# One weight product of a fused attention and bilinear kernel in float32r split parts instead of float32

## The chip, the cores and the metric

The kernel runs on one core of a Trainium2 chip. The metric is the device time of one execution in microseconds (us), the median of three runs. The engines are PE (matrix products), DVE (vector operations), ACT (scalar engine: copies, activations), POOL and SP. SP issues the loads from HBM, ACT issues the stores.

## The reference

An attention block with 8 batches, 8 heads, 512 tokens, 32 state rows and 64 elements per head runs in both directions; its result, 544 rows of 512 per batch, goes through a bilinear block.

```python
scores = scale * x @ state.T;  a = softmax(scores);   xread = a @ state      # 512 rows per batch
scores2 = scale * state @ x.T; a2 = softmax(scores2); sread = a2 @ x         # 32 rows per batch
x = concatenate([xread, sread]) as rows of 512                               # 8 * 544 rows
h = (x @ w1) * (x @ w2) @ w3                                                 # 512 -> 1024 -> 1024
out = h @ w_out                                                              # 1024 -> 512
```

x and state are float32, the four weights come as float64.

## The kernel before

`w3 @ w_out` doesn't depend on x, so the kernel forms it once (`wo`, 8 tiles of 128 rows by 512, `FT` = 8) and multiplies `g = (x @ w1) * (x @ w2)` by it. Large products run in float32r: an operand is split into `hi` (rounded to float32r by a copy on ACT) and `lo` (the rest, a subtraction on DVE), and three products hi·lo, hi·hi, lo·hi are summed. `split` writes such a pair. The product `w3 @ w_out` alone runs on whole float32 operands.

The program has these parts, in this order:

- **Weights.** `to_f32` loads one chunk of 128 x 1024 float64 numbers into a `raw` buffer (SP, 1 MB) and turns their bits into float32: two passes on ACT (line 100 into the destination, line 102 into `ulps`) and two on DVE (lines 103 and 104). There are 20 chunks: 4 of w_out (`convert_wout`), 8 of w3 (`convert_w3`, one for each tile of `wo`) and 8 of w1 and w2 (`convert_quarter`, two for each of four quarters, kept in `w_sb`). Chunks of w_out and the first four of w3 lie in places of `w_sb` that w1 and w2 take later.
- **`w34(i, ks)`** forms tile i of `wo`: eight products 128 x 128 by 128 x 512 (one for each k), summed in a PSUM bank, then split into `wo_hi` and `wo_lo`.
- **Attention of batch 0**, between the tiles of `wo`: `scores` (line 115 on PE, then a chain of DVE and ACT passes up to `at_hi`, `at_lo`), `transpose_a2` (line 185, copied by line 187) and `read_state` (line 197, whose result is scaled into `sread` by eight small ACT operations, line 205).
- **Stage 1 of batch 0** (`stage1`, line 256, 8 tiles of g) by quarters: `sets(q)` multiplies the state by quarter q of w1 and w2 (`sw_hi`, `sw_lo`; line 115), stage 1 multiplies that by `at`; `hidden` makes the product of the two halves and splits it into g. `early_stage2` runs part of stage 2 for two row tiles in between.
- **Stage 2** (`stage2`, `project`, line 266): g by `wo`, four row tiles per batch; the next batch's attention and `sw` (`side_steps`) stand between them.
- **Batches 1 to 7** repeat stage 1 and stage 2. Before the last one, `state_rows` does both stages for the 256 state rows of all batches; its inputs are transposed `sread` (line 408) and split parts of `w_sb` (`grp_z`).

PE and SP run their instructions in the order in which they are written. ACT and DVE are ordered by a scheduler when the program is built, and then run strictly in that order. PSUM has two single banks (`bank`) for `wo` and stage 2 and three double ones (`two_banks`).

Of the kernel before, what the change touches and what calls it, by code (L numbers as in the profile page):

```python
# [21 lines left out]
F32 = mybir.dt.float32  # L22
# [6 lines left out]
P = 128  # L29
NF = 512  # L30
# [3 lines left out]
def attn_bilinear_kernel(  # L34
# [46 lines left out]

    def split(hi, lo, src):

        nc.scalar.copy(out=hi, in_=src)  # L84
        nc.vector.tensor_tensor(out=lo, in0=src, in1=hi.bitcast(F32), op=ALU.subtract)  # L85


    def to_f32(pool, src, out):

        raw = pool.tile([P, NW], mybir.dt.int64, name="raw", bufs=3)
        nc.sync.dma_start(out=raw, in_=src)
        words = raw.bitcast(I32).rearrange("p (n k) -> p k n", k=2)
        high, low = words[:, 1], words[:, 0]
        bits = out.bitcast(I32)
        nc.scalar.activation(out=out, in_=high.bitcast(F32), func=AF.Prelu, scale=2.0**-112, alpha=-(2.0**32))  # L100
        ulps = pool.tile([P, NW], I32, name="ulps", bufs=2)
        nc.scalar.activation(out=ulps, in_=low.bitcast(U32), func=AF.Copy, scale=2.0**-29)  # L102
        nc.vector.tensor_scalar(out=bits, in0=bits, scalar1=3, scalar2=None, op0=ALU.logical_shift_left)
        nc.vector.tensor_tensor(out=bits, in0=bits, in1=ulps, op=ALU.add)  # L104
# [29 lines left out]
    def attention_steps(b):  # L134
        xd = x_tiles[b][0]
        a2 = {}

        def scores():
            ps = two_banks()
            per_head(ps, b, lambda rows, j: xd[rows, j])  # L140
            flat = lambda t: t.rearrange("p k s -> p (k s)")

            s1 = work_tile()
            nc.vector.transpose(out=flat(s1), in_=flat(ps))  # L144

            m2 = att.tile([P, KT], F32, name="m2")
            nc.vector.tensor_reduce(out=m2, in_=ps, axis=AX.X, op=ALU.max)
            nc.vector.tensor_scalar_mul(m2, m2, -SCALE)
            e2 = att.tile([P, KT, S], F32, name="e2", bufs=1)
            sum2 = att.tile([P, KT], F32, name="sum2")  # L150
            for kt in range(KT):
                one = slice(kt, kt + 1)
                nc.scalar.activation(
                    out=e2[:, kt], in_=ps[:, kt], func=AF.Exp, bias=m2[:, one], scale=SCALE, accum_out=sum2[:, one]
                )
            nc.vector.tensor_scalar_add(sum2, sum2, 1e-9)
            nc.vector.reciprocal(out=sum2, in_=sum2)
            a2["e"], a2["sum"] = e2, sum2

            J = KT * S // NS  # L160
            s1v = flat(s1).rearrange("p (j n) -> p j n", n=NS)
            m1 = att.tile([P, J], F32, name="m1")
            nc.vector.tensor_reduce(out=m1, in_=s1v, axis=AX.X, op=ALU.max)
            nc.vector.tensor_tensor(
                out=s1v, in0=s1v, in1=m1.unsqueeze(2).broadcast_to([P, J, NS]), op=ALU.subtract
            )
            nc.scalar.activation(out=s1, in_=s1, func=AF.Exp, scale=SCALE)
            sum1 = att.tile([P, J], F32, name="sum1")
            nc.vector.tensor_reduce(out=sum1, in_=s1v, axis=AX.X, op=ALU.add)  # L169
            nc.vector.tensor_scalar_add(sum1, sum1, 1e-9)  # L170
            nc.vector.reciprocal(out=sum1, in_=sum1)
            nc.vector.tensor_tensor(
                out=s1v, in0=s1v, in1=sum1.unsqueeze(2).broadcast_to([P, J, NS]), op=ALU.mult
            )
            at = work_tile()
            nc.vector.transpose(out=flat(at), in_=flat(s1))
            at_tiles[b] = [att.tile([P, KT, S], F32R, name=f"at_{part}", bufs=1) for part in ("hi", "lo")]
            split(*at_tiles[b], at)

        def transpose_a2():  # L180
            ps = two_banks()
            for kt in range(KT):
                for t in range(NT):
                    ts = slice(t * P, (t + 1) * P)
                    nc.tensor.transpose(out=ps[:, kt, ts], in_=a2["e"][:, kt, ts], identity=ident)  # L185
            a2["t"] = work_tile()
            nc.scalar.copy(out=a2["t"], in_=ps)

        def read_state():

            xs = x_tiles[b][1]
            ps = two_banks()
            for kt in range(KT):
                for t in range(NT):
                    for j in range(NP):
                        mine = slice(j * NS, (j + 1) * NS)
                        nc.tensor.matmul(  # L197
                            ps[mine, kt, :D], a2["t"][:, kt, t * P + j * NS:t * P + (j + 1) * NS],
                            xs[:, t, 2 * j + kt], start=(t == 0), stop=(t == NT - 1),
                        )  # L200
            rows = slice(b % PER * NS, (b % PER + 1) * NS)
            for kt in range(KT):
                for j in range(NP):
                    mine = slice(j * NS, (j + 1) * NS)
                    nc.scalar.activation(
                        out=sread[rows, b // PER, 2 * j + kt, :], in_=ps[mine, kt, :D],
                        func=AF.Copy, scale=a2["sum"][mine, kt:kt + 1],
                    )

        return scores, transpose_a2, read_state  # L210

# [23 lines left out]
        split(*(t[:, :, c * NQ:(c + 1) * NQ] for t in tiles[half, i]), ps)  # L235


    def hidden(ps, n, g_hi, g_lo):
        a_sb = main.tile([P, NF], F32, name="tmp", bufs=4)
        nc.scalar.copy(out=a_sb[:, :n], in_=ps[:, 0, :n])  # L240
        nc.vector.tensor_tensor(out=a_sb[:, :n], in0=a_sb[:, :n], in1=ps[:, 1, :n], op=ALU.mult)  # L241
        split(g_hi, g_lo, a_sb[:, :n])

    def new_g():
        return [main.tile([P, NF], F32R, name=f"g_{part}", bufs=FT) for part in ("hi", "lo")]

    def stage1(b, ft, gs):
        half, c = divmod(ft * P, NF)
        ps = two_banks()
        hi, lo = at_tiles[b]  # L250
        for i in range(2):
            w_hi, w_lo = sw_tiles[b][half, i]
            k = 0
            for kt in range(KT):
                for w, a in ((w_hi, lo), (w_hi, hi), (w_lo, hi)):
                    nc.tensor.matmul(  # L256
                        ps[:, i], w[:, kt, c:c + P], a[:, kt], start=(k == 0), stop=(k == 3 * KT - 1)
                    )
                    k += 1
        gs.append(new_g())  # L260
        hidden(ps, S, *gs[-1])

    def project(ps, gs, tt, ft):
# [26 lines left out]
    def run(steps):  # L290
        for step in steps:
            step()
# [9 lines left out]

    with tc.tile_pool(name="pro", bufs=2) as pro:

        places = [w_sb[:, n // 2, n % 2].rearrange("p j f -> p (j f)") for n in range(2 * QT)]
        w_out = places[FT // 2:]
        w3s, w34_ps = {}, {}

        def convert_wout(j):
            to_f32(pro, wout[j], w_out[j])  # L310

        def convert_w3(i):
            w3s[i] = places[i] if i < FT // 2 else pro.tile([P, NW], F32, name="w3", bufs=2)
            to_f32(pro, w3t[i], w3s[i])

        def w34(i, ks):

            if ks[0] == 0:
                w34_ps[i] = bank()
            ps = w34_ps[i]  # L320
            for k in ks:
                nc.tensor.matmul(  # L322
                    ps[:, :DO], w3s[i][:, k * P:(k + 1) * P], w_out[k // 2][:, k % 2 * DO:(k % 2 + 1) * DO],
                    start=(k == 0), stop=(k == FT - 1),
                )
            if ks[-1] == FT - 1:
                split(wo["hi"][:, i], wo["lo"][:, i], ps[:, :DO])

# [29 lines left out]
                w34(i, ks[2 * j:2 * j + 2])  # L358
        for i in range(2, FT):
            convert_w3(i)  # L360
            w34(i, ks)
            if i == 2:
                load_x(0)
                scores, transpose_a2, read_state = attention_steps(0)
# [9 lines left out]
                convert_quarter(1)  # L374
        for quarter in range(QT):
            stage1(0, 2 * quarter, gs)
            if quarter + 2 < QT:
                convert_quarter(quarter + 2)
            if quarter + 1 < QT:
                sets(quarter + 1)  # L380
            else:
                run(side[0][:1])
            if quarter:
                early_stage2(quarter - 1)
            if quarter == 1:
                load_x(1)
                side = side_steps(1)
            stage1(0, 2 * quarter + 1, gs)
        run(side[0][1:])
        early_stage2(QT - 1)  # L390
        for tt in range(NT):
            dests = [(out[0, tt * P:(tt + 1) * P], 0, P)]
# [9 lines left out]
    def state_rows():  # L402
# [10 lines left out]
        for ft in range(FT):  # L413
            quarter, c = divmod(ft * P, NQ)
            ps = two_banks()
            for i in range(2):
# [4 lines left out]
                for kt in range(NP):  # L421
                    ks = slice(kt * P, (kt + 1) * P)
                    hi, lo = (t[:, kt] for t in sr)
                    for w, a in ((wh, lo), (wh, hi), (wl, hi)):
# [1 line left out]
                            ps[:, i, :n], w[:, ks], a, start=(k == 0), stop=(k == 3 * NP - 1)  # L426
                        )
                        k += 1
            gs.append([g[:, :n] for g in new_g()])
            hidden(ps, n, *gs[-1])  # L430
        for tt in range(n // P):
            stage2(gs, tt, [(out[tt * PER + q, S:], q * NS, NS) for q in range(PER)])
# [1 line left out]

    for b in range(1, B):
        if b == B - 1:
            state_rows()
        gs = []
        for ft in range(FT):
            stage1(b, ft, gs)  # L440
# [43 lines left out]
```

## Time and profile before

| | |
|---|---|
| median of 3 runs | 526.55 us (526.3 to 529.43) |
| profiled execution | 526.63 us |
| its span, first to last instruction | 524.8 us |
| PE busy | 502.5 us, 96% |
| DVE, ACT busy | 266.2 us (51%), 247.2 us (47%) |
| moved by DMA | 47.67 MB, mean 91 GB/s |

PE's busy time has modelled ends, so the places where another engine keeps PE waiting are found in the waits and in the chain of work that ended last. The first 84 us hold all work on the weights; after them the batches repeat.

### The profile page before, as it was taken

To read this page: it belongs to the slowest core of one execution; us is meant where nothing else is said; L and a number is where in the kernel's file an instruction comes from. 1 tells how busy PE (TensorE), PEld (TensorE's weight loads), DVE (VectorE), ACT (ScalarE), POOL (GpSimd) and SP (SyncE) were. 2 spreads that over 40 slices of the span, in tenths; PEclk is the share of its full clock that TensorE was granted. 3 is DMA by queue.
4 is the path that set the end of the run, shared out by engine and by line. 5 is a ranking of instruction groups with operands and counts; after the bars stand their busy time and mean duration, and the time that the engine had idled before them with its cause. 6 is when DMAs were issued, how large, how long until landed. Compare 5 with 4: busy or idle time off the path is not lost.

```text
span 524.8 us, 7504 instructions
## 1 busy us (share of the span) xinstructions
PE 502.5 (96%) x3192; PEld 369.8 (70%) x3192; DVE 266.2 (51%) x352; ACT 247.2 (47%) x403; POOL 0.7 (0%) x6
## 2 busy tenths in 40 slices
PE   1999898999999999999999999999999999999996
PEld 0444346756886788678868886887688777998885
DVE  3648948376155724653464348343915492742410
ACT  5657966245443634453444434443544364632410
POOL 0000000000000000000000000000000000000000
PEclk9999899999999999999999999999999999999999
DMA  8987733021302120321023003300330001001001
GB/s 328 387 335 315 283 136 149 5 81 61 106 0 101 50 97 2 101 101 46 0 106 122 21 1 121 106 21 0 121 121 1 21 22 41 0 1 41 0 33 49
DMA packets 11361, 47.67 MB, mean 91 GB/s; under 512 B 1344, under 2 KB 2368, under 8 KB 6720
## 3 DMA queue, kind: packets, MB, share of 16 engines
q1 hardware_dynamic: 6336, 38.28, 19.7%
q10 hardware_dynamic: 4992, 8.92, 4.6%
q8 instruction: 25, 0.41, 0.3%
q14 instruction: 8, 0.07, 0.0%
HBM read 38.27 MB, written 8.91 MB: 90 GB/s over the span
## 4 chain that ended last, share of the span: by engine, by line
PE 88%; DVE 5%; DMA 3%; ACT 3%; issue 1%; DVEq 0%; ACTq 0%
PE ps_o L266 35%; PE ps L256 32%; PE ps_o L322 7%; PE ps L115 6%; PE ps L425 4%; PE ps L197 2%; PE ps L185 1%; DMA raw<-in_w3t_dram 1%; DMA raw<-in_wout_dram 1%; DMA raw<-in_w_dram 1%; ACT ulps L102 1%; DVE w_sb L104 1%; ACT w_sb L100 1%; DVE sum L169 0%; DVE work L144 0%
## 5 line engine op out<-in xcount | busy, mean ns | idle before, releaser
L266 PE MATMUL ps_o<-wo_lo,g_hi 128*128 128x512 f32 x272 | 108.6, 399 | 1.0 <-ACT g_hi L84 1.0
L241 DVE TENSOR_TENSOR tmp<-tmp,ps 128x512 f32<-128x512 f32 (+1 forms) x72 | 47.3, 657 | 118.6 <-ACT tmp L240 118.6
L266 PE MATMUL ps_o<-wo_hi,g_lo 128*128 128x512 f32 x272 | 106.1, 390 | 0.6 <-DVE g_lo L85 0.6
L266 PE MATMUL ps_o<-wo_hi,g_hi 128*128 128x512 f32 x272 | 106.0, 390 | 0.0
L256 PE MATMUL ps<-at_lo,sw_hi 128*128 128x512 f32 x256 | 100.2, 392 | 1.7 <-DVE tmp L241 1.7
L256 PE MATMUL ps<-at_hi,sw_lo 128*128 128x512 f32 x256 | 99.6, 389 | 0.0
L256 PE MATMUL ps<-at_hi,sw_hi 128*128 128x512 f32 x256 | 99.6, 389 | 0.0
L240 ACT COPY tmp<-ps 128x512 f32<-128x512 f32 (+1 forms) x72 | 40.5, 562 | 63.9 <-PE ps L256 63.0
L85 DVE TENSOR_TENSOR g_lo<-tmp,g_hi 128x512 fp32r<-128x512 f32 (+1 forms) x72 | 47.6, 661 | 41.6 <-ACT g_hi L84 41.5
L84 ACT CAST g_hi<-tmp 128x512 fp32r<-128x512 f32 (+1 forms) x72 | 43.0, 597 | 47.3 <-DVE tmp L241 47.0
L266 PEld LDWEIGHTS ps_o<-wo_lo,g_hi 128*128 128x128 f32 x272 | 51.0, 188 | 19.4 <-issue 7.5
L278 ACT COPY tmp<-ps_o 128x512 f32<-128x512 f32 x34 | 19.9, 586 | 85.8 <-PE ps_o L266 85.8
L266 PEld LDWEIGHTS ps_o<-wo_hi,g_lo 128*128 128x128 f32 x272 | 51.0, 188 | 12.0 <-DVE g_lo L85 1.1
L266 PEld LDWEIGHTS ps_o<-wo_hi,g_hi 128*128 128x128 f32 x272 | 51.1, 188 | 9.8
L256 PEld LDWEIGHTS ps<-at_lo,sw_hi 128*128 128x128 f32 x256 | 48.1, 188 | 12.4 <-DVE tmp L241 2.2
L256 PEld LDWEIGHTS ps<-at_hi,sw_hi 128*128 128x128 f32 x256 | 48.1, 188 | 10.1 <-issue 0.2
L256 PEld LDWEIGHTS ps<-at_hi,sw_lo 128*128 128x128 f32 x256 | 48.0, 188 | 10.0
L322 PE MATMUL ps_o<-w_sb 128*128 128x512 f32 x64 | 30.3, 635 | 11.7 <-DVE w_sb L104 11.6
L85 DVE TENSOR_TENSOR sw_lo<-ps,sw_hi 128x1024 fp32r<-128x1024 f32 (+1 forms) x36 | 39.3, 1096 | 4.3 <-ACT sw_hi L84 3.8
L84 ACT CAST sw_hi<-ps 128x1024 fp32r<-128x1024 f32 (+1 forms) x36 | 32.8, 918 | 11.5 <-PE ps L115 11.4
L322 PEld LDWEIGHTS ps_o<-w_sb 128*128 128x128 f32 x64 | 12.9, 205 | 28.3 <-issue 14.7
L115 PE MATMUL ps<-w_sb,st 64*32 64x512 f32 (+1 forms) x576 | 31.5, 546 | 0.0
(54 smaller groups left out, 434.6 us busy)
## 6 DMA issues: line engine op xcount, KB each, us to landing
raw<-in_w3t_dram SPq DMA_DIRECT2D x8, 1024.0 KB, 6.7
x_d<-in_x_d_dram SPq DMA_DIRECT2D x8, 1024.0 KB, 5.7
x_s<-in_x_s_dram SPq DMA_DIRECT2D x8, 1024.0 KB, 5.8
raw<-in_w_dram SPq DMA_DIRECT2D x8, 1024.0 KB, 4.9
out_dram<-tmp ACTq DMA_DIRECT2D x32, 256.0 KB, 2.0
raw<-in_wout_dram SPq DMA_DIRECT2D x4, 1024.0 KB, 6.6
st<-in_st_dram SPq DMA_DIRECT2D x8, 64.0 KB, 4.9
out_dram<-tmp ACTq DMA_DIRECT2D x8, 64.0 KB, 1.7
```

The lines of the kernel that those rows point to most:

```text
L84: nc.scalar.copy(out=hi, in_=src)
L85: nc.vector.tensor_tensor(out=lo, in0=src, in1=hi.bitcast(F32), op=ALU.subtract)
L100: nc.scalar.activation(out=out, in_=high.bitcast(F32), func=AF.Prelu, scale=2.0**-112, alpha=-(2.0**32))
L115: nc.tensor.matmul(ps[j * NS:(j + 1) * NS, q], sts[b][rows, j], moving(rows, j), start=True, stop=True)
L197: nc.tensor.matmul(ps[mine, kt, :D], a2["t"][:, kt, t * P + j * NS:t * P + (j + 1) * NS], xs[:, t, 2 * j + kt], start=(t == 0), stop=(t == ...
L240: nc.scalar.copy(out=a_sb[:, :n], in_=ps[:, 0, :n])
L241: nc.vector.tensor_tensor(out=a_sb[:, :n], in0=a_sb[:, :n], in1=ps[:, 1, :n], op=ALU.mult)
L256: nc.tensor.matmul(ps[:, i], w[:, kt, c:c + P], a[:, kt], start=(k == 0), stop=(k == 3 * KT - 1))
L266: nc.tensor.matmul(ps[:, :DO], g, wo[w][:, ft, :], start=(ft == 0 and k == 0), stop=(ft == FT - 1 and k == 2))
L278: nc.scalar.copy(out=o, in_=ps[:, :DO])
L322: nc.tensor.matmul(ps[:, :DO], w3s[i][:, k * P:(k + 1) * P], w_out[k // 2][:, k % 2 * DO:(k % 2 + 1) * DO], start=(k == 0), stop=(k == FT ...
L425: nc.tensor.matmul(ps[:, i, :n], w[:, ks], a, start=(k == 0), stop=(k == 3 * NP - 1))
```

## The change

`w3 @ w_out` now runs as the other large products do: each chunk of w3 and of w_out is converted in one of four places of `w_sb` and then split, w_out into pairs with the buffers of g, w3 into pairs with the buffers of `sw`. Each of the 64 float32 products becomes three float32r products. The buffers of g are now pairs of two tiles. `raw` has four buffers, not three. The last tile of `wo` is formed in two halves, with stage 1's first tile between them. `scores` of batch 1 stands after stage 1's last tile, not before it. `read_state` scales its result in one DVE operation and moves it into `sread` with four DMAs from POOL's queue. The instructions of `state_rows` may not be issued before the last split of the batch ahead of it.

```diff
     def split(hi, lo, src):
-        nc.scalar.copy(out=hi, in_=src)
-        nc.vector.tensor_tensor(out=lo, in0=src, in1=hi.bitcast(F32), op=ALU.subtract)
+        return (
+            nc.scalar.copy(out=hi, in_=src),
+            nc.vector.tensor_tensor(out=lo, in0=src, in1=hi.bitcast(F32), op=ALU.subtract),
+        )
...
-        raw = pool.tile([P, NW], mybir.dt.int64, name="raw", bufs=3)
+        raw = pool.tile([P, NW], mybir.dt.int64, name="raw", bufs=4)
...
+            scaled = att.tile([P, KT, D], F32, name="scaled")
+            nc.vector.tensor_tensor(
+                out=scaled, in0=ps[:, :, :D], in1=a2["sum"].unsqueeze(2).broadcast_to([P, KT, D]), op=ALU.mult
+            )
             rows = slice(b % PER * NS, (b % PER + 1) * NS)
-            for kt in range(KT):
-                for j in range(NP):
-                    mine = slice(j * NS, (j + 1) * NS)
-                    nc.scalar.activation(
-                        out=sread[rows, b // PER, 2 * j + kt, :], in_=ps[mine, kt, :D],
-                        func=AF.Copy, scale=a2["sum"][mine, kt:kt + 1],
-                    )
+            for j in range(NP):
+                nc.gpsimd.dma_start(
+                    out=sread[rows, b // PER, j * KT:(j + 1) * KT], in_=scaled[j * NS:(j + 1) * NS]
+                )
...
-    def new_g():
-        return [main.tile([P, NF], F32R, name=f"g_{part}", bufs=FT) for part in ("hi", "lo")]
+    def g_pair():
+        return [main.tile([P, 2, NF], F32R, name=f"g_{part}", bufs=FT // 2) for part in ("hi", "lo")]
...
-        places = [w_sb[:, n // 2, n % 2].rearrange("p j f -> p (j f)") for n in range(2 * QT)]
+        places = [w_sb[:, n // 2, n % 2].rearrange("p j f -> p (j f)") for n in range(FT // 2, FT)]
...
+        def convert(src, parts):
+            place = places[(len(w_outs) + len(w3s)) % len(places)]
+            to_f32(pro, src, place)
+            split(*parts, place.rearrange("p (k f) -> p k f", f=NF))
+            return parts
...
+            w_hi, w_lo = w3s[i]
             for k in ks:
-                nc.tensor.matmul(
-                    ps[:, :DO], w3s[i][:, k * P:(k + 1) * P], w_out[k // 2][:, k % 2 * DO:(k % 2 + 1) * DO],
-                    start=(k == 0), stop=(k == FT - 1),
-                )
+                o_hi, o_lo = (t[:, k % 2] for t in w_outs[k // 2])
+                for n, (w, o) in enumerate(((w_hi, o_lo), (w_hi, o_hi), (w_lo, o_hi))):
+                    nc.tensor.matmul(
+                        ps[:, :DO], w[:, k * P:(k + 1) * P], o, start=(k == 0 and n == 0),
+                        stop=(k == FT - 1 and n == 2),
+                    )
...
-            w34(i, ks)
+            w34(i, ks if i < FT - 1 else ks[:FT // 2])
...
             stage1(0, 2 * quarter, gs)
+            if quarter == 0:
+                w34(FT - 1, ks[FT // 2:])
...
             if quarter + 1 < QT:
                 sets(quarter + 1)
-            else:
-                run(side[0][:1])
...
-        run(side[0][1:])
+        run(side[0])
...
         if b == B - 1:
-            state_rows()
+            with tc.issue_after(last_split[0].ins), tc.issue_after(last_split[1].ins):
+                state_rows()
```

Lines below the changed `split` stand one or two lines further down in the changed kernel up to `read_state`: its lines 85 and 86 are `split`, 102 and 104 the ACT passes of `to_f32`, 105 and 106 its DVE passes.

Three places show what the scheduler made of it. The first is ACT at tiles 2 to 4 of `wo`. Before, `ps_o_157` is tile 2 and `ps_o_181` tile 3, and `raw_174`, `raw_228`, `raw_258` are the chunks of w3 for tiles 3, 4 and 5:

```order
L84 CAST wo_hi_80<-ps_o_119 128x512
L100 ACTIVATE w_sb_77<-raw_174 128x1024
L102 ACTIVATE ulps_177<-raw_174 128x1024
L84 CAST wo_hi_80<-ps_o_157 128x512
L100 ACTIVATE w3_227<-raw_228 128x1024
L102 ACTIVATE ulps_231<-raw_228 128x1024
L100 ACTIVATE w3_257<-raw_258 128x1024
L102 ACTIVATE ulps_261<-raw_258 128x1024
```

The same stretch of ACT in the changed kernel, where `ps_o_217` is tile 2, `sw_hi_250` is the high part of w3's chunk for tile 3, and `raw_325` and `raw_374` are the chunks for tiles 4 and 5:

```order
L85 CAST wo_hi_80<-ps_o_143 128x512
L102 ACTIVATE w_sb_77<-raw_252 128x1024
L104 ACTIVATE ulps_255<-raw_252 128x1024
L85 CAST wo_hi_80<-ps_o_217 128x512
L85 CAST sw_hi_250<-w_sb_77 128x1024
L102 ACTIVATE w_sb_77<-raw_325 128x1024
L104 ACTIVATE ulps_328<-raw_325 128x1024
L102 ACTIVATE w_sb_77<-raw_374 128x1024
L104 ACTIVATE ulps_377<-raw_374 128x1024
L85 CAST sw_hi_323<-w_sb_77 128x1024
```

The cast that gives PE tile 3's weights stands behind the cast of tile 2's finished result.

The second place is DVE in the second half of batch 0's `scores`, from the sum of the exponentials to the second transposition. Before:

```order
L169 TENSOR_REDUCE sum_216<-work 128x32
L85 TENSOR_TENSOR wo_lo<-ps_o,wo_hi 128x512
L170 TENSOR_SCALAR sum_216<-sum_216 128x32
L103 TENSOR_SCALAR w_331<-w_331 128x1024
L171 RECIPROCAL sum_216<-sum_216 128x32
L104 ISA w_331<-w_331,ulps 128x2048
L172 TENSOR_TENSOR work<-work,sum_216 128x1024
L103 TENSOR_SCALAR w_sb<-w_sb 128x1024
L176 STREAM_TRANSPOSE work<-work 128x1024
```

The same stretch in the changed kernel:

```order
L171 TENSOR_REDUCE sum_312<-work 128x32
L106 ISA w_sb<-w_sb,ulps 128x2048
L172 TENSOR_SCALAR sum_312<-sum_312 128x32
L106 ISA w_sb<-w_sb,ulps 128x2048
L173 RECIPROCAL sum_312<-sum_312 128x32
L105 TENSOR_SCALAR w_sb<-w_sb 128x1024
L174 TENSOR_TENSOR work<-work,sum_312 128x1024
L86 TENSOR_TENSOR wo_lo<-ps_o,wo_hi 128x512
L178 STREAM_TRANSPOSE work<-work 128x1024
```

Two passes of the long kind (line 106) stand in it where one (line 104) stood, and one short pass less. In the first half, from the first transposition on, the order before has one short and one long pass; the changed one has two short ones, one long one and a `wo_lo` subtraction. Over both halves the changed chain has one long pass and one `wo_lo` subtraction more.

The third place is ACT ahead of the last tile of `wo` in the changed kernel: `ps_o_474` is tile 6, `raw_673` and `raw_680` are chunks of w1 and w2 of the last quarter, `sw_hi_501` and `sw_hi_514` are `sets(0)`, and `sw_hi_541` is the high part of w3's chunk for tile 7:

```order
L104 ACTIVATE ulps_676<-raw_673 128x1024
L85 CAST wo_hi_80<-ps_o_474 128x512
L104 ACTIVATE ulps_683<-raw_680 128x1024
L85 CAST sw_hi_501<-ps_2_503 128x2x256
L85 CAST sw_hi_514<-ps_2_516 128x2x256
L85 CAST sw_hi_541<-w_sb_77 128x1024
```

The same place before, from tile 6's result (`ps_o_339`) on; tile 7 then needs nothing more from ACT:

```order
L84 CAST wo_hi_80<-ps_o_339 128x512
L84 CAST sw_hi_350<-ps_2_352 128x2x256
L84 CAST sw_hi_363<-ps_2_365 128x2x256
L100 ACTIVATE w_sb_77<-raw_429 128x1024
L100 ACTIVATE w_sb_77<-raw_436 128x1024
```

The cast of tile 7's chunk is the last of four ACT operations that stand behind tile 6's result.

More of the change, by code (lines that the diff above doesn't have):

```diff
@@ L235, in sw_quarter @@
         split(*(t[:, :, c * NQ:(c + 1) * NQ] for t in tiles[half, i]), ps)
+    last_split = []
     def hidden(ps, n, g_hi, g_lo):
@@ L241, in hidden, with new_g @@
         nc.vector.tensor_tensor(out=a_sb[:, :n], in0=a_sb[:, :n], in1=ps[:, 1, :n], op=ALU.mult)
-        split(g_hi, g_lo, a_sb[:, :n])
-    def new_g():
-        return [main.tile([P, NF], F32R, name=f"g_{part}", bufs=FT) for part in ("hi", "lo")]
+        last_split[:] = split(g_hi, g_lo, a_sb[:, :n])
+    def g_pair():
+        return [main.tile([P, 2, NF], F32R, name=f"g_{part}", bufs=FT // 2) for part in ("hi", "lo")]
+    g_pairs = {}
+    def new_g(ft):
+        if ft % 2 == 0:
+            g_pairs["now"] = g_pair()
+        return [g[:, ft % 2] for g in g_pairs["now"]]
     def stage1(b, ft, gs):
@@ L259, in stage1 @@
                     k += 1
-        gs.append(new_g())
+        gs.append(new_g(ft))
         hidden(ps, S, *gs[-1])
@@ L303, in attn_bilinear_kernel @@
     with tc.tile_pool(name="pro", bufs=2) as pro:
-        places = [w_sb[:, n // 2, n % 2].rearrange("p j f -> p (j f)") for n in range(2 * QT)]
-        w_out = places[FT // 2:]
-        w3s, w34_ps = {}, {}
+        places = [w_sb[:, n // 2, n % 2].rearrange("p j f -> p (j f)") for n in range(FT // 2, FT)]
+        w_outs, w3s, w34_ps = {}, {}, {}
+        def convert(src, parts):
[3 more added lines that the diff above has]
+            return parts
         def convert_wout(j):
-            to_f32(pro, wout[j], w_out[j])
+            w_outs[j] = convert(wout[j], g_pair())
         def convert_w3(i):
-            w3s[i] = places[i] if i < FT // 2 else pro.tile([P, NW], F32, name="w3", bufs=2)
-            to_f32(pro, w3t[i], w3s[i])
+            w3s[i] = [t.rearrange("p k f -> p (k f)") for t in convert(w3t[i], sw_pair())]
         def w34(i, ks):
@@ L428, in state_rows @@
                         k += 1
-            gs.append([g[:, :n] for g in new_g()])
+            gs.append([g[:, :n] for g in new_g(ft)])
             hidden(ps, n, *gs[-1])
```

## Prediction

> **What bounds the kernel now.** I read the waits of PE first, because PE is busy nearly throughout and its busy time is modelled. The columns are the wait in all, how often, the longest (us):
>
> ```profile
> PE ps_o L322 <- DVE w_sb L104: 11.6, 1, 11.6
> PE ps L197 <- ACT work L187: 2.3, 1, 2.3
> PE ps L256 <- DVE tmp L241: 1.7, 1, 1.7
> PE ps_o L266 <- ACT g_hi L84: 1.0, 1, 1.0
> PE ps L408 <- DVE grp_lh L85: 0.8, 1, 0.8
> PE ps_o L266 <- DVE g_lo L85: 0.6, 1, 0.6
> ```
>
> These are all: 18.0 us, 11.6 of them before the first product. PE works through one fixed order, so the span is its issue time plus these waits. An edit that shortens neither on PE is worth nothing. Next, busy time by stretch: start and end, length, then busy us (and count) of PE, PEld, DVE, ACT, POOL, then granted clock, DMA share, GB/s.
>
> ```profile
> 5.60:17.70 12.10, 6.04 (x8) 2.38 (x8) 7.68 (x8) 9.52 (x9) 0.00 (x0) 1.00 0.99 376
> 17.70:42.00 24.30, 24.30 (x64) 10.59 (x70) 14.10 (x16) 14.92 (x16) 0.00 (x0) 1.00 0.92 366
> 42.00:60.00 18.00, 15.83 (x57) 6.94 (x56) 16.98 (x23) 14.92 (x19) 0.00 (x0) 1.00 0.78 307
> 60.00:83.40 23.40, 21.68 (x172) 10.84 (x172) 15.06 (x19) 17.46 (x28) 0.00 (x0) 0.93 0.56 217
> ...
> 137.00:441.00 304.00, 304.00 (x2066) 232.94 (x2065) 154.90 (x198) 137.59 (x241) 0.00 (x0) 1.00 0.17 61
> ```
>
> From 137 on PE is never short of work. In the weights' part the bound changes: PE alone from 17.7 to 42, DVE from 42 to 60 (16.98 of 18.00 busy), where attention's passes and the conversion share it. The chain of work that ended last says the same (start, length, what):
>
> ```profile
> 17.70 24.31 PE ps_o L322 x56
> ...
> 44.94 1.16 DVE work L144
> ...
> 56.88 1.16 DVE work L176
> ...
> 60.08 1.43 PE ps L197 x64
> 61.51 8.37 PE ps_o L322 x16
> ...
> 83.48 5.74 PE ps L256 x24
> ...
> 136.66 21.98 PE ps L256 x96
> ...
> 187.57 21.76 PE ps L256 x96
> ```
>
> **The products.** A float32 product stands as two records. 56 records in 24.31 us are 0.434 us each, 0.868 per product; 96 float32r matmuls of the same shape in 21.76 us are 0.2267, three of them 0.680. For 64 products that is 64 x 0.188 = 12.0 us less on PE, the whole gain if PE were the bound of all of them.
>
> **What the split adds.** Twelve chunks each get a cast on ACT and a subtraction on DVE, 128 x 1024, SBUF to SBUF. `at_hi` and `at_lo` are such operations (start, length):
>
> ```profile
> 5.60 1.12 ACT L100 ACTIVATE w_sb<-raw 128x1024 f32<-128x1024 f32 x1 [3.59 <-DMA raw<-in_wout_dram]
> 6.62 1.13 ACT L102 ACTIVATE ulps<-raw 128x1024 int32<-128x1024 uint32 x1
> ...
> 58.07 1.04 ACT L84 CAST at_hi<-work 128x1024 fp32r<-128x1024 f32 x1 [1.11 <-DVE work L176]
> 59.02 1.00 ACT L187 COPY work<-ps 128x1024 f32<-128x1024 f32 x1
> 59.93 0.59 ACT L84 CAST wo_hi<-ps_o 128x512 fp32r<-128x512 f32 x1
> ```
>
> ```profile
> 57.96 1.18 DVE L104 CUSTOM_DVE_ANT_0 w_sb<-w_sb,ulps 128x2048 uint16<-128x2048 uint16 x1
> 59.07 0.68 DVE L103 TENSOR_SCALAR w_sb<-w_sb 128x1024 int32<-128x1024 int32 x1
> 59.66 1.22 DVE L85 TENSOR_TENSOR at_lo<-work,at_hi 128x1024 fp32r<-128x1024 f32 x1
> 60.80 0.69 DVE L85 TENSOR_TENSOR wo_lo<-ps_o,wo_hi 128x512 fp32r<-128x512 f32 x1
> ```
>
> From start to start a cast takes 0.95, a pass of the conversion on ACT 1.03, a cast of 512, by the same overlap of 0.09, 0.5; on DVE a subtraction 1.14, the long pass 1.1, the short one 0.6, and `wo_lo`, of the same length, 0.6. So 12 x 0.95 = 11.4 us go onto ACT and 12 x 1.14 = 13.7 us onto DVE, all before the last tile of `wo`. I now walk four points where PE's order meets the other engines.
>
> *Scores of batch 0 (before: 42.0, where the 56 records end).* A chunk takes ACT 2 x 1.03 + 0.95 = 3.0 us. Seven chunks (four of w_out, three of w3) from 5.60 end at 26.6; the seventh's cast waits for its last DVE pass (1.23) and takes 1.04: 28.9. PE, still on the first two tiles, starts tile 2 at about 30.7: 24 x 0.2267 = 5.44, to 36.2. Tile 3's cast stands behind `wo_hi` of tile 2, which waits for that; behind the pair wait the conversions of tiles 4 and 5. Cast 36.9 to 38.0, so PE waits 1.8, and 0.8 more for the low part; 5.44 later tile 3 is done: 44.4. **+2.4.** The fourth raw buffer brings nothing under this: 1 MB at the 376 GB/s of the first stretch takes 2.8 us, and ACT now needs 3.0 for each chunk; with ACT idle it would be worth no more than the chunks' waiting time in the first 17.7 us, 12.1 - 9.5 = 2.6 us.
>
> *Read of the state (before: 60.08).* The scores take 1.0; DVE then has tile 4's and 5's subtractions and `wo_lo` ahead of the first transposition, which starts at about 46.6 (before 44.94). From it to the end of the second one took 58.04 - 44.94 = 13.1; the changed order has one long pass and one `wo_lo` more, 1.7: 61.4. Then the cast 0.95, the copy 1.05, and up to 0.8 that ACT holds ahead of the two: 64.2. **+4.1.** PE has its tiles 4 and 5 done at about 58 and waits 6 us.
>
> *Second tile of stage 1 (before: 83.48).*
>
> ```profile
> 70.58 1.07 ACT L84 CAST sw_hi<-ps 128x512 fp32r<-128x512 f32 x2
> ```
>
> 64.2 + 1.43 for the read + 5.44 for tile 6 and 1.7 for the closed clock (below) = 72.8. Behind tile 6's result on ACT stand its cast 0.5, one conversion pass 1.03, `sets(0)` 1.07, then tile 7's cast 1.04, with 0.4 to start: 76.8. PE waits about 2.8 after its own sets. Half of tile 7 takes 2.72 and a wait of 0.8 for the low part, stage 1's first tile 2.72, the other half 2.72, `sets(1)` 1.02: 86.8, 87.0 with seams. **+3.5.** The 1.7 us that line 256 waited for `tmp` is inside: the half tile covers it.
>
> *Batch 1's stage 1 (before: 136.66).* PE's own work between is the same. The waits for g (1.0 + 0.6) go with the scores. Late next is the copy that frees the first early bank for row tile 2: on ACT it now stands behind the scores' two exponentials, and those wait for DVE:
>
> ```profile
> 113.59 0.69 ACT L153 ACTIVATE e<-ps,m 128x512 f32<-128x512 f32 x1 [3.50 <-DVE m L148]
> ```
>
> That puts PE's wait between none and 3.5 + 2 x 0.7 = 4.9; the two `sw` and the last early products (5 us of PE) cover over half, and I take 2.1. **+0.5**, so 4.0 in all.
>
> *The rest is nothing.* From 137 PE waits once, 0.8. A pair of g is freed three matmuls (0.7 us) later than one tile was, under the 12 matmuls (2.72) of the next stage 1 tile. The eight scale operations leave ACT (0.3 each), where no one waited:
>
> ```profile
> L205 ACT ACTIVATE sread<-ps,sum 32x64 f32<-32x64 f32 x64 | 19.5, 305 | 4.1 <-PE ps L197 3.3
> ```
>
> `issue_after` keeps `grp_z` out of the weights' part, two casts and two subtractions; none is awaited there. **Sum:** span 524.8 + 4.0 = 528.8; the profiled execution took 526.63, 1.83 more than its span, and stands 0.08 above the median: 530.6 us.
>
> **The clock.** The weights' loads on PE stand 0.85 us apart at the start and 0.43 later; after the wait at 58 the clock falls again:
>
> ```profile
> 12.60 0.34 PEld L322 LDWEIGHTS ps_o<-w_sb 128*128 128x128 f32 x1 [0.52 <-issue]
> 13.45 0.34 PEld L322 LDWEIGHTS ps_o<-w_sb 128*128 128x128 f32 x1 [0.52 <-issue]
> ...
> 18.24 0.19 PEld L322 LDWEIGHTS ps_o<-w_sb 128*128 128x128 f32 x1 [0.24 <-issue]
> 18.67 0.19 PEld L322 LDWEIGHTS ps_o<-w_sb 128*128 128x128 f32 x1 [0.24 <-issue]
> ```
> ```profile
> 60.00:70.00 10.00, 9.92 (x88) 4.83 (x96) 4.45 (x5) 7.19 (x15) 0.00 (x0) 0.83 0.49 184
> ```
>
> A mean of 0.83 over 10 us is 3.4 us at half, 1.7 us lost, after a wait of 2.3. I keep that one in the sum. The Trainium skill, TensorE: Matmul & The Clock Gate (Why this matters for your kernels), says to leave no idle gaps above about 3 us between bursts. By that only the 6 us wait would close the clock, and the sum would stay; this trace closed it after 2.3, so the 2.8 may count too.
>
> **The rivals.**
> - *The engines pack well.* ACT was busy 9.52 + 14.92 + 14.92 = 39.4 us from 5.6 to 60; with 11 casts, 10.5, it could be through at 55.5. DVE: 7.68 + 14.10 + 16.98 + 11 x 1.14 = 51.3 from 6.75, 58.0. Then the read of the state starts at 59, and without the waits of 2.8 and 0.8 stage 1's second tile at 78.2, all told 5 us sooner, **522 us**. Against it: the orders are fixed, and PE's results stand ahead of casts that PE needs. The full 12 us are out of reach, as DVE would need to be through seven us before that.
> - *Slower by the clock.* The waits at tile 3 (1.8 + 0.8) and before tile 7 (2.8) close it as the 2.3 did, 1.7 us each, and the closed start lasts one spell longer: + 3 to 5, **535 us**. It decides as soon as a wait above some 2 us falls into one of the clock's spells.
> - *POOL's DMAs come late.* For the last `read_state` the first of four must land before line 408:
>
> ```profile
> 434.35 1.03 PE ps L197 x64
> 435.38 5.68 PE ps_o L266 x24
> ```
>
>   5.7 us cover it. No POOL transfer stands in the trace; four one after the other at the 1.7 us of the nearest stores and at the 4.9 of `st` are 6.8 and 19.6:
>
> ```profile
> out_dram<-tmp ACTq DMA_DIRECT2D x8, 64.0 KB, 1.7
> st<-in_st_dram SPq DMA_DIRECT2D x8, 64.0 KB, 4.9
> ```
>
>   The fourth is awaited last, and they overlap in the queue; I take nothing, at worst a wait of 1 to 4: **533 us**. The Trainium skill, DMA: Bandwidth & Descriptors (Anatomy of one DMA), gives 2.0 us plus bytes over 436 GB/s for one from this queue: as an estimate 8.2 us for four in a row, a wait of 2.5.
> - *Neither way.* Gains and waits cancel, or the three products take PE as long as one did, while its waits stay as they are: **526.5**. For it speaks only that both terms are near 12 us.
>
> **How the numbers follow.** A measurement here tells about 1%, 5.3 us, from no change: 521.3 and 531.8 are the bounds. Forecast 0.46 (528 to 533, by 1 us of hold-up on ACT and DVE at each point, a third of it over the bound); packed 0.22 (519 to 525, nearly half past the bound); cancelled 0.10; clock 0.17; late DMAs 0.05. Faster 0.10, slower 0.46 x 0.33 + 0.22 = 0.37, the same 0.53. The range leaves out the far end of the packed case and of the clock's: 521 to 536.
>
> **What would show it.** Scores start near 44.5, the read of the state near 64 behind a PE wait of about 6 us for the copy of `work`, tile 7 behind a wait for its cast; DVE and ACT over 90% busy from 45 to 75; everything after 141 moved as a block. If the wait before the read is under 3 us, the walk of DVE's queue is wrong, and the result is nearer to 522. If PE waits at line 408 for a DMA, POOL's rival holds.

## The result, and the profile after

The changed kernel took 532.79 us (median of 8 runs, 529.84 to 534.82), the kernel before beside it 526.49 (8 runs); the ratio is 1.0109, with a 95% interval of 1.0087 to 1.0132. Forecast were 530.6 and a range of 521 to 536. The profiled execution took 534.3 with a span of 532.3, 7.5 above that of before; it is one of the two longest of the eight, 1.5 above their median, at a mean granted clock of 0.980, where four of the eight had 0.986.

The waits of PE come first again (wait in all, how often, the longest):

```profile
PE ps_o L342 <- ACT sw_hi L85: 17.3, 3, 13.1
PE ps L199 <- ACT work L189: 5.6, 1, 5.6
PE ps_o L342 <- DVE g_lo L86: 2.2, 1, 2.2
PE ps_o L278 <- ACT tmp L290: 1.8, 1, 1.8
PE ps L428 <- DVE grp_lh L86: 0.8, 1, 0.8
PE ps_o L342 <- DVE sw_lo L86: 0.5, 1, 0.5
```

They sum to 28.2 us against 18.0 before. The new ones are for results of the split or of what queues with it: `sw_hi`, `sw_lo`, `g_lo`, and the copy of `work` ahead of the state's read, which waits 5.6 us in place of 2.3. One is not, the 1.8 us for `tmp`, a copy that frees the early bank: it comes with the later scores, as an experiment below shows.

The chain that ended last, at the places that the prediction walks (start, length, what):

```profile
36.85 1.06 ACT sw_hi L85
37.93 1.24 DVE sw_lo L86
39.21 6.86 PE ps_o L342 x22
46.07 1.02 PE ps L117 x16
...
62.73 1.03 ACT at_hi L85
63.76 0.92 ACT work L189
64.73 1.94 PE ps L199 x64
66.67 7.38 PE ps_o L342 x24
...
75.70 1.92 ACT sw_hi L85 x3
...
78.92 4.63 PE ps_o L342 x10
...
90.26 5.66 PE ps L268 x24
```

PE goes from cast to subtraction to products, as forecast. But 22 products take 6.86 us at 39, 24 take 7.38 at 66 and 10 take 4.63 at 79: 0.31, 0.31 and 0.46 each, where the prediction had 0.2267. Stretches of 10 us show why. The columns are start and end, length, busy us of PE, PEld (PE's weight loads), DVE, ACT and POOL, then the granted clock (the mean share of PE's full clock), the DMA share and GB/s:

```profile
30.00:40.00 10.00, 7.71 (x30) 5.38 (x30) 5.67 (x7) 6.28 (x8) 0.00 (x0) 0.97 0.74 311
40.00:50.00 10.00, 10.00 (x50) 7.24 (x49) 9.24 (x10) 8.91 (x10) 0.00 (x0) 0.86 0.64 235
50.00:60.00 10.00, 9.11 (x45) 7.29 (x43) 9.76 (x16) 8.86 (x13) 0.00 (x0) 1.00 0.76 292
60.00:70.00 10.00, 5.27 (x72) 4.42 (x73) 10.00 (x12) 9.18 (x10) 2.09 (x4) 0.67 0.75 277
70.00:80.00 10.00, 7.36 (x54) 4.79 (x54) 8.03 (x10) 7.77 (x9) 0.00 (x0) 0.84 0.67 262
80.00:90.00 10.00, 10.00 (x65) 7.57 (x63) 3.41 (x5) 1.89 (x5) 0.00 (x0) 0.81 0.00 0
...
120.00:130.00 10.00, 8.21 (x68) 4.83 (x68) 9.12 (x12) 6.44 (x11) 0.00 (x0) 0.91 0.41 154
130.00:140.00 10.00, 10.00 (x69) 6.96 (x68) 6.69 (x8) 4.28 (x5) 0.00 (x0) 0.92 0.08 32
```

A mean of 0.86 over 10 us is 1.4 us that the clock withheld. Over these rows it is 0.3 + 1.4 + 3.3 + 1.6 + 1.9 + 0.9 + 0.8 = 10.2 us, against the 1.7 of before. So the ledger of the two profiled executions reads: 12.0 us less in products (the prediction's term, not measured apart), 10.2 more in waits, 8.5 more in closed clock, together + 6.7. The spans differ by 7.5; the 0.8 left is not assigned. The clock's share is an upper figure, because it counts closed time in which PE was waiting too (half of 60 to 70). It is also that of one execution: at a mean granted clock of 0.986, as in four of the eight, some 3 us less are withheld (0.006 of 532). Experiments below weigh it.

Behind 83.4 PE waits twice more, 1.8 and the 0.8 that stood before too, and after 145 the two kernels run alike.

### The profile page after: what moved, and what is told of

Read it like the earlier page. It is cut to its first block, busy times and chain, and to the rows that moved or that the text cites. A ratio compares the mean times of both kernels' runs of the same rounds, so it can differ in the third digit from the quotient of the medians.

```text
span 532.3 us, 7653 instructions
## 1 busy us (share of the span) xinstructions
PE 499.9 (94%) x3256; PEld 387.9 (73%) x3256; DVE 281.7 (53%) x372; ACT 238.5 (45%) x351; POOL 16.5 (3%) x38
## 3 DMA queue, kind: packets, MB, share of 16 engines
q0 software_dynamic: 1024, 0.53, 0.3%
## 4 chain that ended last, share of the span: by engine, by line
PE 91%; ACT 5%; DVE 1%; DMA 1%; issue 1%; SPq 0%; ACTq 0%
PE ps_o L278 36%; PE ps L268 33%; PE ps_o L342 7%; PE ps L117 7%; PE ps L445 4%; PE ps L199 2%; PE ps L187 2%; ACT sw_hi L85 1%; DMA raw<-in_w3t_dram 1%; ACT ulps L104 1%; ACT w_sb L102 1%; DVE sw_lo L86 0%; DVE w_sb L106 0%; ACT g_hi L85 0%; ACT tmp L290 0%
## 5 line engine op out<-in xcount | busy, mean ns | idle before, releaser
L278 PEld LDWEIGHTS ps_o<-wo_hi,g_lo 128*128 128x128 f32 x272 | 51.4, 189 | 11.2
L342 PE MATMUL ps_o<-g_lo,sw_hi 128*128 128x512 f32 x64 | 29.7, 464 | 19.7 <-ACT sw_hi L85 17.3
L86 DVE TENSOR_TENSOR sw_lo<-ps,sw_hi 128x1024 fp32r<-128x1024 f32 (+1 forms) x36 | 39.2, 1096 | 0.5
L342 PEld LDWEIGHTS ps_o<-g_lo,sw_hi 128*128 128x128 f32 x64 | 14.0, 218 | 25.8 <-ACT sw_hi L85 18.2
```

The source lines that it names most:

```text
L278: nc.tensor.matmul(ps[:, :DO], g, wo[w][:, ft, :], start=(ft == 0 and k == 0), stop=(ft == FT - 1 and k == 2))
L342: nc.tensor.matmul(ps[:, :DO], w[:, k * P:(k + 1) * P], o, start=(k == 0 and n == 0), stop=(k == FT - 1 and n == 2),)
```

## The experiments

The median of before was 526.5 to 526.8 in every comparison, so the medians may be set beside each other. My theory: the chunks' casts and subtractions, in the queues of ACT and DVE, hold PE back, and its waits then close the clock. The rivals: the small edits cost the time (scores later, GpSimd's DMAs), or the clock costs it alone.

**The small edits alone.** To the kernel before were added only the new `read_state`, as in the change, and the later scores:

```diff
-            else:
-                run(side[0][:1])
...
-        run(side[0][1:])
+        run(side[0])
```

> Before with the small edits alone: scores of batch 1 later, the state's read through one DVE operation and GpSimd's DMAs; w3 w_out stays a float32 product with no split. My theory, that the time went to the split's operations on ACT and DVE and to the clock behind the waits: the small edits cost nothing, 525 to 528, first wait of the scores' bank as before, waits of PE about 18 us in all. Rival, that the moved scores and GpSimd's DMAs cost it: 530 to 533, with a wait of PE at batch 1's stage 1 or at the state's rows.

It took 526.85 us, ratio 1.0012 (0.9988 to 1.0036): these two edits cost nothing, and that rival is out. The scores' new place has the wait for the copy of the early bank, 1.8 us, and lost the 1.0 + 0.6 for g, so it is even. GpSimd's DMAs cost nothing; in the changed kernel they stand so (the issue of the last four; then packets, KB each, median us to landing):

```profile
443.81 1.96 POOL L209 DMA_DIRECT2D sread<-scaled  x4 [48.73 <-DVE scaled L204]
sread<-scaled POOLq DMA_DIRECT2D x32, 16.0 KB, 4.7
```

**The half tile too.** The same, with the second half of the last tile of `wo` behind stage 1's first tile. The pairs of g buffers and the hold on `state_rows` are as in the changed kernel. The product is float32 with no split; `raw` has three buffers, and the chunks lie as before.

```diff
-            w34(i, ks)
+            w34(i, ks if i < FT - 1 else ks[:FT // 2])
...
+            if quarter == 0:
+                w34(FT - 1, ks[FT // 2:])
```

> Before (float32 product, no split) with the small edits and the last tile's second half behind stage 1's first tile; attention where it was. If the half tile covers the wait of 1.5 to 2 us for tmp and no more: 524 to 526, with the read's wait of 2.3 left. If the later attention of the version that took 521 did nothing and the half tile all: 521.

523.98 us, 0.9945 (0.9917 to 0.9973), 2.9 less than without. Its waits of PE:

```profile
PE ps_o L345 <- DVE w_sb L106: 11.5, 1, 11.5
PE ps L199 <- ACT work L189: 2.2, 1, 2.2
PE ps_o L278 <- ACT tmp L290: 1.8, 1, 1.8
PE ps L431 <- DVE grp_lh L86: 0.8, 1, 0.8
```

The wait for `tmp` (2.0 in the version before this one) is gone. So the parts around the split were worth 2.8 us, and the split with its products cost 532.8 - 524.0 = 8.8. The fourth `raw` buffer and the four shared places, which the split's version alone has, are in the 8.8; no run varies them by themselves.

**The split made short.** The changed kernel with casts and subtractions of 128 of the 1024 columns. The three products of each pair stay, of the same shapes, and read those 128 columns again and again.

```diff
-            split(*parts, place.rearrange("p (k f) -> p k f", f=NF))
+            split(*(t[:, 0, :P] for t in parts), place[:, :P])
...
-                o_hi, o_lo = (t[:, k % 2] for t in w_outs[k // 2])
+                o_hi, o_lo = (t[:, 0, :P].unsqueeze(1).broadcast_to([P, 4, P]) for t in w_outs[k // 2])
...
```

> After with the chunks' split cut to 128 of 1024 columns, and those columns standing for all (the product w3 w_out is not the reference's): three float32r matmuls of the same shapes, a cast and a subtraction an eighth as long. If the full-length casts and subtractions are what PE waits for: the waits of 2.2, 0.8 and part of those for tile 3 and tile 7 go, PE's 12 us come through by about two thirds, 521 to 525. What stays is the conversion itself, 2 x 1.03 us on ACT and 1.7 on DVE a chunk: waits of 3 to 4 near 35 and before the read of the state. If the clock or the small edits are the cause whatever the split costs: 529 or more.

524.09 us, 0.9948 (0.9925 to 0.9971): 8.7 less than the changed kernel, so without the full-length casts and subtractions, and what follows from them in waits and clock, the loss is gone; the fourth `raw` buffer and the four places stayed. But it only draws level with the float32 product (523.98). In the median the 12 us of PE came to nothing even with the split nearly free:

```profile
PE ps_o L342 <- ACT sw_hi L85: 17.4, 3, 12.1
PE ps L199 <- ACT work L189: 3.8, 1, 3.8
PE ps_o L278 <- ACT tmp L290: 1.8, 1, 1.8
PE ps L428 <- DVE grp_lh L86: 0.8, 1, 0.8
PE ps_o L342 <- DVE g_lo L86: 0.3, 1, 0.3
```
```profile
50.00:60.00 10.00, 6.20 (x81) 5.07 (x83) 10.00 (x15) 9.62 (x12) 0.00 (x0) 0.89 0.71 268
60.00:70.00 10.00, 9.04 (x72) 6.55 (x64) 8.26 (x12) 6.85 (x8) 2.61 (x4) 0.77 0.87 320
70.00:80.00 10.00, 8.95 (x32) 7.04 (x33) 5.25 (x8) 3.89 (x7) 0.00 (x0) 0.83 0.02 9
```

Waits of 24.1 us against 16.3 are 7.8 more, the closed clock of the three rows 1.1 + 2.3 + 1.7 = 5.1 against 1.7 is 3.4 more: 11.2 of the 12. PE caught up with the conversion, and waited for that, in two ways. Before the state's read (3.8 us) DVE was full, 10.00 of 10.00 from 50 to 60. Before tile 3 (3.3 of the 17.4) it was the order: ACT idled 2.9 us for the cast of tile 2's result, behind which the next conversion pass of tile 3's chunk stood, and DVE idled 2.8.

```profile
32.08 0.58 ACT L85 CAST wo_hi<-ps_o 128x512 fp32r<-128x512 f32 x1 [2.90 <-PE ps_o L342]
32.56 1.13 ACT L104 ACTIVATE ulps<-raw 128x1024 int32<-128x1024 uint32 x1
```

**One engine's part left out.** First without the subtractions, the high part standing for the low one too (below); then without the casts, one DVE addition in each subtraction's place writing a part that stands for both.

```diff
-            split(*parts, place.rearrange("p (k f) -> p k f", f=NF))
-            return parts
+            nc.scalar.copy(out=parts[0], in_=place.rearrange("p (k f) -> p k f", f=NF))
+            return [parts[0], parts[0]]
```

> After without the twelve subtractions of the chunks on DVE; the high parts stand in for the low parts (w3 w_out is not the reference's), so PE's matmuls and ACT's twelve casts stay. If the two engines hold PE together: tile 7's wait falls by some 2 us and the first product starts 0.5 sooner, but the read of the state still waits near 6 us, since DVE's own attention passes wait for what ACT hands on: 526 to 530. If DVE alone holds PE, 13.7 us less on it give back most of PE's 12: 520 to 523. If neither does and the clock or the small edits are the cause: 532.

> After without the twelve casts of the chunks on ACT; one DVE addition in each subtraction's place writes a part that stands for both (w3 w_out is not the reference's). ACT loses 11.4 us, DVE keeps its load, PE its matmuls. If the two engines hold PE together: tile 7's wait falls by about 1 us and the read's stays near 6 to 7, 527 to 532, less gained than without the subtractions. If ACT alone holds PE: 522 to 525.

530.17 (1.0062, 1.0036 to 1.0087) and 530.30 (1.0071, 1.0039 to 1.0102): 2.6 and 2.5 less, just above 526 to 530 and within 527 to 532, which were expected if the two engines hold PE together, and far from either engine alone. Their waits before the read were 6.3 and 6.6 us, no shorter. The two parts together are worth 8.7, more than both single gains; taking one away leaves the other in PE's path.

**The queue before tile 7.** The conversion of the third and fourth quarter of w1 and w2 queued behind tile 7's cast and subtraction:

```diff
-                convert_quarter(quarter + 2)
+                with tc.issue_after(chunk_split[0].ins), tc.issue_after(chunk_split[1].ins):
+                    convert_quarter(quarter + 2)
```

> After with the conversion of the third and fourth quarter of w1 and w2 queued behind the last chunk's cast and subtraction, on ACT and DVE alike. By the walk of ACT's queue, a conversion pass and sets(0) stand ahead of tile 7's cast: its wait should fall from near 4.5 us to about 2 and the second tile of stage 1 come 2 to 3 sooner, 528 to 531; less still, 526 to 528, if with the wait the clock's closing at 77 goes too. If the order there is not what holds PE: 532 as after, or more by what stage 1 then waits for its w1 and w2.

529.12 us, 1.0054 (1.0028 to 1.0081), 3.7 less. In its profile the second tile of stage 1 starts at 85.92 in place of 90.26, and 70 to 80 has a granted clock of 1.00. The walk of ACT's queue at this point is borne out for the wait itself: tile 7's wait for its cast fell from 2.6 to 1.75 us, but 0.5 for its low part came instead. Most of the 4.3 us at the second tile is the clock, which is open here from 40 to 50 and from 70 to 90, though at tile 3 PE waits 1.6 and 0.5 us as it does in the changed kernel. All waits together are 28.3 us, against 28.2.

**The clock.** Two versions put float32r matmuls of 128x512 into PE's waits, their results unused: first 20 before the state's read, then also 7 before tile 3 and 10 before tile 7.

```diff
+            if i in {3: 7, 7: 10}:
+                fill({3: 7, 7: 10}[i])
             w34(i, ks if i < FT - 1 else ks[:FT // 2])
...
             elif i == 5:
+                keep_warm(20)
                 read_state()
```

> After with 20 more float32r matmuls of 128x512 (4.5 us of PE's time, into a bank nobody reads) ahead of the state's read of batch 0, inside the wait of 5.6 us. They take no wait away. If the closed clock behind that wait is what the prediction missed: the spell from 63 to 70 goes, about 3.4 us less, 527 to 530. If the clock follows something else than PE's waits: 532 as after, or up to 1 us more by matmuls that reach past the wait.

531.96 us, 1.0111 (1.0061 to 1.0162): no gain that can be told from nothing, which by itself speaks against the clock. The read stood at 64.8, the wait before it was 1.1, and 60 to 70 had the full clock. But 40 to 50 still had 0.83 and 70 to 80 0.88, and tile 7 waited for the same casts. With all three filled:

> After with float32r matmuls of 128x512 into banks nobody reads in three of PE's waits: 7 before tile 3, 20 before the read of the state, 10 before tile 7. No data comes sooner. The one filler at the read moved the read not at all and the time by some 1 us. If the clock's closings behind the waits at 36 and 75 take the rest, all three spells up to 85 go and the time is 526 to 529; if the engines' queues alone hold PE, 531 to 533, since what a faster PE gains it then waits for again.

528.08 us, 1.0035 (1.0015 to 1.0055), 4.7 less than the changed kernel, with 37 matmuls more whose results nobody reads:

```profile
60.00:70.00 10.00, 8.85 (x99) 7.10 (x98) 10.00 (x13) 9.67 (x10) 3.11 (x4) 1.00 0.76 297
70.00:80.00 10.00, 8.95 (x65) 6.16 (x65) 8.98 (x11) 6.49 (x8) 0.00 (x0) 1.00 0.58 234
```

Stage 1's second tile starts at 84.98, 5.3 sooner. So of the 8.8 us that split and products cost, the clock's closings carry near 4.7 and the queues the rest.

Each run has a mean granted clock, so runs with the same one can be compared, few as they are:

| mean granted clock | kernel | runs, us |
|---|---|---|
| 0.986 | changed | 532.2 to 532.9 (4) |
| 0.986 | w1 and w2 queued later | 530.7 to 531.5 (4) |
| 0.986 | split made short | 525.0, 525.9 |
| 0.992 | changed | 529.8 |
| 0.992 | half tile, float32 | 525.9, 526.0 |
| 0.993 | split made short | 522.3 to 522.5 (3) |

At the same clock the full-length casts and subtractions cost about 7 us, the cheaper product brings about 3 of its 12, and the two together lose about 4 to the float32 version. That the changed kernel's clock closes more often is the rest of the 8.8, which agrees with the 4.7. The short split draws level with the float32 version because its clock closes more often too (0.9895 against 0.996 in the median). And of the 3.7 us from the queue before tile 7 less than 2 remain. These are estimates: a mean clock does not say where it was closed.

**Attention later.** Nothing but the state's rows at the end needs the read of batch 0. In the changed kernel its transposition went behind tile 5 and its read behind the first half of tile 7:

```diff
-            elif i == 3:
-                scores()
-            elif i == 4:
-                transpose_a2()
-            elif i == 5:
-                read_state()
+            for slot, step in ((3, lambda: scores()), (5, lambda: transpose_a2()), (7, lambda: read_state())):
+                if slot == i:
+                    step()
+            if i == 5:
                 convert_quarter(0)
```

> After with batch 0's attention later: transposition behind tile 5, read of the state behind tile 7. The split stays. If the wait before the read is DVE's load of attention in the midst of the conversion: that wait goes, but waits of about 2 at tiles 6 and of 4 at tile 7 show instead, since the chunks' casts and subtractions are still to be done: read or not, stage 1's second tile comes 2 to 3 us sooner, 528 to 531. If the order of the attention were the whole trouble, all 12 us of PE would come through: 520 to 522, as the version with the float32 product gave.

529.55 us, 1.0046 (1.0025 to 1.0066), 3.2 less. The wait before the read is gone, and the waits for `sw_hi` grew from three (17.3 us) to four (20.1). The split is awaited wherever attention stands. The same edit without the split, on the version with the half tile:

> Before (float32 product, no split) with the small edits, the second half of the last tile of wo behind stage 1's first tile, and the steps of batch 0's attention later: transposition behind tile 5 and read of the state behind tile 7, in place of 4 and 5. If DVE's queue from 42 to 60 is what PE waits for, and nothing but the state's rows at the end needs the read: the waits of 2.3, 1.7 and the scores' 1.0 and 0.6 go and nothing takes their place, and the clock stays open, 519 to 522. If DVE's load only comes due later, a wait of 2 to 4 us appears at tile 6, at sets(0) or at stage 1: 524 to 527.

521.15 us, 0.9891 (0.9853 to 0.9929); each of its four runs is below all ten of the version with the half tile. Here nothing takes the place of the waits that went; these are all:

```profile
PE ps_o L345 <- DVE w_sb L106: 11.4, 1, 11.4
PE ps_o L278 <- ACT tmp L290: 1.8, 1, 1.8
PE ps L432 <- DVE grp_lh L86: 0.8, 1, 0.8
```

**One tile split.** On that version w_out's parts were made where ACT and DVE have room, and the fifth tile alone taken in three products; the read of batch 0 moved one tile forward, behind tile 6. The loop below runs over all four chunks:

```diff
+        parted = (4,)
...
+            if i in parted:
+                w3s[i] = [t.rearrange("p k f -> p (k f)") for t in part(sw_pair(), w3s[i])]
...
+            if i in (2,):
+                for j in ((0, 1) if i == 2 else (2, 3)) if False else range(4):
+                    w_outs[j] = part(g_pair(), w_out[j])
```

> The version that took 521, with w_out's split put where ACT and DVE are idle (behind the third tile's conversion, 17 to 42 us) and one of the eight tiles, the fifth, as three float32r products; the read of the state behind tile 6. Five casts and five subtractions in place of twelve, 8 x 0.188 = 1.5 us less for PE. If a split pays where the two engines have room: PE waits as little as without, 518 to 520. If any split's operations come back as waits: 521 to 524, with a wait of 1 to 3 us at tile 5 or before the read.

520.15 us, 0.9849 (0.9815 to 0.9883), the fastest run here. Against the 0.9891 without any split the intervals overlap, so that the one tile pays is not shown; a wait of 1.1 for `wo_lo` came with it, and the profile without any split has a closed clock of 1.7 us (0.83 from 110 to 120) where this one has none. The result lies between the two that were expected.

## Why the prediction was near, and where it fell short

- *Scores of batch 0:* forecast 44.4, measured 46.07. The wait for tile 3's cast and low part came as walked (1.6 + 0.5 us in the rows below, 1.8 + 0.8 forecast). The walk's own terms add to 44.2. What it left out is that the clock closed on it; the loss of 1.7 is the difference.

```profile
35.94 0.39 PE L342 MATMUL ps_o<-g_hi,sw_lo 128*128 128x512 f32 x1
37.95 0.50 PE L342 MATMUL ps_o<-g_lo,sw_hi 128*128 128x512 f32 x1 [1.62 <-ACT sw_hi L85]
38.29 0.40 PE L342 MATMUL ps_o<-g_hi,sw_hi 128*128 128x512 f32 x1
39.21 0.59 PE L342 MATMUL ps_o<-g_hi,sw_lo 128*128 128x512 f32 x1 [0.53 <-DVE sw_lo L86]
39.60 0.63 PE L342 MATMUL ps_o<-g_lo,sw_hi 128*128 128x512 f32 x1
40.03 0.63 PE L342 MATMUL ps_o<-g_hi,sw_hi 128*128 128x512 f32 x1
```

  From 39.60 to 42.6 the starts stand 0.43 us apart, in place of 0.23.
- *Read of the state:* forecast 64.2 behind a wait of about 6 us, measured 64.73 behind 5.6. The place and the size are right, but in part by luck. DVE's second transposition ended at 62.68, forecast 61.4, partly because the late tile 3 kept DVE waiting 0.45 us for `wo_hi`. ACT's passes ahead of the cast ended with it, at 62.73, so the 0.8 that the walk allowed for ACT was not needed. DVE was busy over 92% from 40 to 70 and ACT 89 to 92%; from 70 to 80 both were less busy than forecast, 80 and 78%.
- *Second tile of stage 1:* forecast 87.0, measured 90.26. Tile 7's cast was forecast at 76.8 and the three casts end at 77.62, so the queue was right within a microsecond. The 2.4 us left are the clock, 1.6 + 1.9 in the two rows from 70 to 90; the wait of 0.8 that was forecast for the low part is hidden under it. PE's wait for the cast was 2.6 (forecast 2.8, though its own terms give 3.0). Without the one closing that it kept (1.7), the prediction's walk gives 85.3; the version with its waits filled has 84.98.
- *Batch 1's stage 1:* a wait of 2.1 forecast for the copy of the early bank, 1.8 measured; a closed clock of 0.9 + 0.8 behind it was not foreseen. The stage's second part begins at 144.4, forecast 140.7.
- *The rest:* as forecast, nothing. GpSimd's DMAs are not awaited at the state's rows, where the wait is 0.8 as before: that rival is out. By the Trainium skill, DMA: Bandwidth & Descriptors (Anatomy of one DMA), the estimate was 8.2 us for four in a row; here four were issued in 1.96 us, a DMA landed in 4.7 (median), and no wait for them shows.

**The step that fell short is the term of the clock.** The sum kept one closing, 1.7 us, and gave further ones, 3 to 5 us, a chance of 0.17; the profiled execution had them at four places (one of them the one kept), 10.2 us in all, and with the waits filled the median is 4.7 lower, 528.1, near the 528.9 that the forecast is without its one closing. The forecast case and that rival thus both hold in part: the queues give the order and the places, the clock the last few us. The Trainium skill, TensorE: Matmul & The Clock Gate (Why this matters for your kernels), puts the limit at gaps above about 3 us; at 38 it closed behind two waits of 1.6 and 0.5, with two matmuls between them, and the measurement decides.

One reading of the prediction can be sharpened. It booked 12.0 us less on PE as a gain that the split's work then takes back. With the split short, most of the gain was still not there: the conversion alone, by its place behind PE's own results at tile 3 and by DVE's full queue before the read, makes a faster PE wait, and the waits close the clock.

## What to carry to other kernels

Before a product is made cheaper, see what the engine does with the time at the next place where it waits: here 12 us of PE brought nothing in the median even with the split short, since PE then waited for the conversion and the waits closed the clock, and moving work that nobody needs soon (0.9945 to 0.9891) was worth more. Count each new wait of PE like those here (1.6 us and up) with a possible closed clock of 1.7 us behind it, and test that share by filling the wait with matmuls whose result nobody reads. Compare runs at the same granted clock before a gain is put down to an edit. Where two engines each carry half of an added cost, taking away one half shows little; take away both before a cause is dismissed.

## What the runs showed of the hardware

- Whether a wait closes the clock is not set by its length alone. The same wait of 1.8 us for the copy of the early bank ends at 115.4 in the version that took 521.15, with a mean granted clock of 0.83 over 10 us (a loss of 1.7), and at 119.1 in the one with the half tile, with 1.00 before and after:

```profile
110.00:120.00 10.00, 8.21 (x41) 5.83 (x26) 9.86 (x15) 5.19 (x9) 0.00 (x0) 0.83 0.42 156
...
110.00:120.00 10.00, 8.21 (x72) 4.74 (x71) 7.68 (x10) 5.96 (x11) 0.00 (x0) 1.00 0.29 105
120.00:130.00 10.00, 10.00 (x73) 7.07 (x72) 8.23 (x10) 4.75 (x6) 0.00 (x0) 1.00 0.21 80
```

  At tile 3 the waits of 1.6 and 0.5 us, which end at 39.2 in the changed kernel and leave 0.86 from 40 to 50, end at 39.7 in the version with w1 and w2 queued later and leave 1.00:

```profile
38.41 0.50 PE L343 MATMUL ps_o<-g_lo,sw_hi 128*128 128x512 f32 x1 [1.62 <-ACT sw_hi L85]
39.67 0.49 PE L343 MATMUL ps_o<-g_hi,sw_lo 128*128 128x512 f32 x1 [0.53 <-DVE sw_lo L86]
...
40.00:50.00 10.00, 10.00 (x56) 7.35 (x55) 9.47 (x11) 10.00 (x11) 0.00 (x0) 1.00 0.78 271
```

  Runs of one kernel spread in such steps: the changed kernel's fastest took 529.84 us at a mean granted clock of 0.992, its slowest 534.82 at 0.980. The Trainium skill, TensorE: Matmul & The Clock Gate (What's actually happening), calls the gate's window free-running, which agrees with this; no run here moves a wait against the window alone.
- Matmuls that do nothing can shorten a kernel: 37 of them, 8.4 us of PE at 0.2267, took 4.7 us off the median.
